# A new fixed instruction list for chunk-selected attention followed by an ELU MLP

## The chip, the core and the metric

The kernel runs on one core of a Trainium2 chip. A core has five instruction queues that run beside one another: TensorE (PE, matmuls), VectorE (DVE), ScalarE (ACT), GpSimd (POOL) and SyncE (SP, which here only starts DMAs). The metric is the device time of one execution in microseconds (us). Three runs of the kernel before took 292.13, 289.8 and 289.86, median 289.86.

## What is computed

The inputs are q, k and v, each 4 batches x 8 heads x 768 positions x 64 in float32, and two MLP weights, 512 x 2048 and 2048 x 512. The keys of a head are cut into 24 chunks of 32. A query sees only the 6 chunks whose upper bound is highest, among those that are not in its future:

```python
ub = np.sum(np.maximum(q * k_min, q * k_max), axis=-1)      # per query and chunk
ub = np.where(causal, ub, -1000000000.0)
top_chunks = np.argsort(ub, axis=-1)[..., -top_k:]
scores = scale * np.matmul(q, k.transpose(0, 1, 3, 2))
attn = softmax(np.where(mask, scores, -1000000000.0))       # mask: selected and not in the future
x = attn @ v                                                # heads joined to 512 columns
h = x @ w_in
g = np.where(h > 0.0, h, np.exp(np.minimum(h, 0.0)) - 1.0)
out = g @ w_out
```

## The kernel before, in words

The 3072 positions are worked off in eight units of 384. Units 0 and 1 hold the first and second quarters of batches 0 and 1 (192 positions of each batch); units 2 and 3 the second halves of these batches; units 4 to 7 the two halves of batches 2 and 3. A unit goes through preparation, selection, attention and the MLP.

Preparation (`prep_pair` L375, `prep` L519) loads keys and queries by DMA, turns them with matmuls against an identity (kT and qT, L403 for the first quarter units, L544 for the others), takes the least and greatest key of each chunk on DVE (kmin, kmax, L368), copies the turned keys and queries to where the score matmuls read them (kt, ka, qt, qa: the copy helper, L321 on ACT, L323 on DVE and POOL) and makes the positive part of the queries (qr, L343 or L345). Batches 2 and 3 take the bounds from a second load of the keys (`bounds_batch` L473: kc, kminc, kmaxc, kj on DVE at L485 to L500, then the transpose kw on PE at L507).

Selection (`select` L580) forms the upper bounds on PE (ub, L593), turns them on DVE (ubT, L604), finds the sixth largest of each query (max, L612), compares (lt, L617), turns the result back (sT, L621) and copies it as rows of mask beside the queries (mk, L321 on ACT, L323 on DVE and POOL). The first quarters see all their chunks and need no selection.

Attention (`attend_pair` L698, `attend` L760) has score matmuls (L721, L775), an exponential on ACT (ex, L728, L790, L794), a triangle of zeros and ones multiplied in on the diagonal (tri, L733, L807, on DVE or POOL), the weighted sums on PE (pv, L747, L826), and the division on DVE (rcp L637, on L639). The result is transposed for the MLP: on PE (px, L662, then a copy xt) in units 0 and 1, by a transposing DMA (xd, L650) in the others.

The MLP (`mlp` L837) has 16 first products a unit, each of four 128 x 384 matmuls into one PSUM bank (h, L844). Each is followed by an exponential on ACT (e, L851), one subtraction on POOL or DVE (m, L853) and a gate on DVE (g, L857). Twelve groups of four 128 x 512 matmuls (o, L865) make the output in three banks, which are copied out (oe, L321 on ACT or L323 on DVE) and stored by SP.

Nothing decides the order while the kernel runs. The operations are first recorded as a graph; `ORDER` (L39) is a written list of three-letter entries, the first letter the engine, the other two the number of the operation; `PLACES` (L103) gives the buffer numbers. The loop at L917 walks the list and issues each operation, so each engine's queue has the order of its entries. Waits between engines follow from the data and from the reuse of buffers, eight PSUM banks among them. Operations that can run on several engines (m, tri, mk, qa, ka, ky, oe and other copies) take the engine that their entry names.

```python
    with tc.manual_schedule():
        for j in range(0, len(order), 3):
            o = g.ops[64 * DIGITS.index(order[j + 1]) + DIGITS.index(order[j + 2])]
            ...
            o.emit({"P": PE, "A": ACT, "D": DVE, "G": POOL, "S": SP}[order[j]])
```

Fillers (L902) are matmuls of zeros against zeros, 256 columns wide, whose result nobody reads; 170 are recorded and the list names 33 of them. The list has PE 625 entries, ACT 476, DVE 469, POOL 242 and SP 155. The MLP weights are loaded by DMAs that POOL issues (w_in in three pieces, L292; w_out in four, L298), with their conversion to bf16.

Of the kernel before, what the change touches and what calls it, by code (L numbers as in the profile page):

```python
# [39 lines left out]
D00S0rA0sG09D01D03A0tS0yD0iA0WG0mS0wD0kA0uD0eD0qG0bS0vD0cG0aA0VG04S0xG05G0jPjRPjSPjTPjUPjVPjWP1j  # L40
A02P1yS0zP1oP1kG0lP0DS0XG0hP0TD0EG06S0YP0MD0HA0UG08G0oS0+G0fP0KD0NP11G0pD0FA0LA15D0OP1lS0BG0AD0Q
P1aA1nS2fD12P1pP1uA1mD17P1qD1cS0ZA1eP18D1bA0SP1hS2iG1gD13A19G0dA1iS2gP1tD0CA1sP1vGmwD10S2vP1NP1D
P1zA1xG0gP26P1AA1rA0JP25P1XP1EA0-S2ID27D28S2hA1wD1FP1SP1YD1GGmvA1BP1HS2PP1RP1IA1CP1OD1JP29G1dP1+
D1KG0GA0RGmxD1PA16G0nGmyS2OPjXPjYPjZPj-Pj+Pk0Pk1Pk2Pk3Pk4Pk5Pk6Pk7Pk8Pk9PkaPkbPkcP2BG14G1fP2aP1L
GmzD2bD2cP20P2oS2QD1TD21D1UP2dA2sD1ZD22A2FD1-A1MD1QD2tPkdPkePkfPkgP23D2HP1VD2pA24A2GD1WD2qA2ePm-
D0ID2CPmSAm+AmTPkhPkiPkjPkkPklP2JS2RDmUP2wDmVA2KD2DPmWA2LG2MD2rA2xGn0G0PDn1PmKG2EG2SD2yPmOPmGAmP
AmXPmCGmQA2uGmYP3lDmRAmHAmLG2zDmZPn2GmID3mGmMDmJPnyAn3GmAD3nAmDPnaDmNAnzD3pGmEPnuAbkG2AD3oAnbPnm
A2NGnAD3qPneG2jD3rS3fPniDn4S2kA3sDnBAnvDmFS2mP3HAnnGncDn5A3tPn6GnwDndAnjGnoP41A3vDnxPnPG07A42Dnp
GmBA3IDnkP3JP2XDnlA3KPnID2YAnfG3LD2+An7P4FP4DD2ZA4GPnqD3uDn8P3+AnrP4jDn9PnJA40GnsA4EGngP4lDntP38
A4mG4HDnhPnQS2TD31S32G30PnCD3aD39G2-P33P3gD34PnRS4+D3hA36G37S2VPnKA35D3iD3bA3cS50A4kP3wA3jG4nA3e  # L50
PnDD3yS4-A2nD3AG3kPnEA2UD3xG2lS4YD3zPnLG3dD3BG2WP4JD3CS4ZPnSAnMD3GA3ED3DD43P3NP3MS4XDnTP4MP4IP4a
A4ND3FP44D3OP45A4bD3PP4OS57P3QD46A4PP48PnFS7QA3RD4QA49D47S7OP3SP4sA3TP4oD4cP4pP4SA4tP4RP4uG3UShx
D4TP4dP5QD4UA4vP4eD4qP5fD4fG4wP3WD4gSnUP3VA5gP5rD3XA5RP4hD4KG5jS55P5EA5sD4LP4yG5iA4iP4xD3YP4VD4z
G5uP3ZD4AA4WP5xD4rA5FP58D5tA3-P4BD5yG5IP5kA5BP5JD4CG5HAnGD5mPoBG7RA5oD5cSnHPnZA5NG7PD5KS7SA5GPop
D5LA5OS7ND5aAn-PodA5UD5zS51Gn+Po1A5SD59G5TAoCDo0PoJAoqD5lGoDSaBAoePo5D5MG5AAo2D5nDoEGorPohA5eGof
S7UAoKPoxGo3A5pDogS5wPnVAo6DosGoLS7IAoyD5bDo4Po9Go7AoiS8hDoMA5hGozPolDo8AoaGojPotAnWDoASaFGobAom
DokP5VScPGnXA56DocGonAouS53DnYA52G5DDooScRPoFA5CG7TD5WPp6D5XGovAoGD5YG5qS7KPp7G5dD5ZGoHPo+SnOD5-
PoVSnNDowPoWD5+S7LPp0D60A61G62DoIPoXD5vP6gDaGP6cP6iA6hP6mP6eDaHP6lA6dPp8A6fDaJA6nP6aP64A6jPp1D54
G6oSaKA65D6kA6bP66P68P6yA67PoNA69A6zP6wP6qA6xP6GAoOP6pA6HP6uGoPPoRD6rA6vD6sG5PP6ADoQS6tAoSP74P6L
P6MDaIA6BP6IGoTA75P7aP79DoUPp9SazA6JA7bD6KS7MP6EA6NP6YD63P6CP76DpaA6FS7JPoYG6OA77DaLA6DG7cP6-P7A  # L60
P6QA6ZDaMG78A6+P70P6PAoZP6UP72D6RA71P6WSo-DaOP7zA73Pp2A6VSaXA7BP7uDp3P7wA6XP7oP7dG7CA7xD6SSp4P7s
P7mA7vDaNP7kSpbP7eA7lS6TG7yP8cD7fA7tP7qD7gP7iA7pP85D8dA7nP8uS7hA7jP7VD87G8gP8iA7rD86P7EA8yDbeP7D
# [891 lines left out]
```

## Time and profile before

| | before |
|---|---|
| median of three runs | 289.86 us |
| span of the profiled execution, first to last instruction | 287.8 us |
| what the median has beyond this span | 2.1 us |
| granted TensorE clock, mean of the core | 1.000 |
| HBM read and written | 30.41 MB and 6.29 MB |

The profiled execution's own time is known by its span alone; sums are made against the 287.8 us and the 2.1 us are added for the median. In the lines shown below, a group's row gives the line of the code, engine and operation, names and shapes, count, then busy time and the mean duration of one in ns, then the engine's idle time just before these instructions and what ended it. A row of the chain of waits gives start, length and what filled that piece of the path. A row of waits gives the engine and line that waited, what ended the wait, the total in us, how often, and the longest. A row of a DMA says how many KB it moved and the median time from issue to landing.

### The profile page before, as it was taken

What the parts mean: (1) busy time and instruction counts of PE and PEld (TensorE: products, weight loads), DVE (VectorE), ACT (ScalarE), POOL (GpSimd) and SP (SyncE); (2) the same over time, 40 slices, a digit from 0 to 9 for tenths busy, and PEclk for the clock granted to TensorE, in tenths of its full rate; (3) what the DMA queues carried; (4) which work ended last, traced back from release to release, by engine and by line L of the source; (5) the groups of instructions that cost most, each with busy time, mean ns of one, the idle gap of its engine ahead of it and who ended that gap; (6) DMA issues with size and microseconds to landing.
All of it is one profiled execution on the core that took longest, in us unless ns stands there. A gap on an engine that the chain in (4) does not pass through costs nothing.

```text
span 287.8 us, 6917 instructions
## 1 busy us (share of the span) xinstructions
PE 271.3 (94%) x2429; PEld 164.3 (57%) x2429; DVE 218.6 (76%) x637; ACT 213.4 (74%) x472; POOL 140.8 (49%) x271
## 2 busy tenths in 40 slices
PE   6998989999999879999798998999999999999995
PEld 3665555685465745567464544567555656565642
DVE  4628796879969999959898999747997698623850
ACT  2576786789499998889999449987886959891712
POOL 8483845277635668752387616620464135420400
PEclk9999999999999999999999999999999999999999
DMA  8999999939957699999753369604700220023102
GB/s 164 195 217 207 197 218 222 233 83 223 216 141 159 164 204 192 202 250 192 195 114 90 90 135 210 155 18 120 198 3 0 43 87 0 2 65 103 38 2 109
DMA packets 106963, 39.25 MB, mean 136 GB/s; under 512 B 98480, under 2 KB 102576, under 8 KB 106928
## 3 DMA queue, kind: packets, MB, share of 16 engines
q1 hardware_dynamic: 100464, 33.93, 57.1%
q0 software_dynamic: 3696, 4.19, 8.6%
q10 hardware_dynamic: 2768, 0.69, 1.3%
q8 instruction: 19, 0.31, 0.5%
q14 instruction: 16, 0.13, 0.2%
HBM read 30.41 MB, written 6.29 MB: 128 GB/s over the span
## 4 chain that ended last, share of the span: by engine, by line
PE 65%; DVE 20%; ACT 5%; DMA 4%; issue 3%; POOL 2%; DVEq 0%; POOLq 0%; ACTq 0%
PE bank L865 22%; PE bank L844 20%; PE bank L775 8%; PE bank L826 5%; DVE gT L857 4%; PE bank L403 2%; PE bank L593 2%; POOL m L853 2%; DVE thr L612 2%; DMA f<-in_q_dram 2%; DVE on L639 2%; PE bank L544 2%; ACT pt L790 1%; DVE kst L368 1%; DVE kn L494 1%
## 5 line engine op out<-in xcount | busy, mean ns | idle before, releaser
L865 PE MATMUL bank<-w_out_sb,gT 128*128 128x512 bf16 x384 | 92.3, 379 | 0.3 <-DVE gT L857 0.2
L844 PE MATMUL bank<-xt,w_in_sb 128*128 128x384 bf16 x512 | 89.5, 326 | 3.3 <-DMA xt<-on 1.8
L853 POOL TENSOR_SCALAR m<-e 128x384 f32<-128x384 f32 x107 | 56.2, 536 | 58.0 <-ACT e L851 47.7
L851 ACT ACTIVATE e<-bank 128x384 f32<-128x384 f32 x128 | 58.6, 492 | 19.4 <-PE bank L844 17.7
L844 PEld LDWEIGHTS <-w_in_sb 128*128 128x128 bf16 x512 | 49.3, 98 | 38.9 <-issue 7.3
L857 DVE SCALAR_TENSOR_TENSOR gT<-bank,m 128x384 bf16<-128x384 f32 x128 | 65.6, 549 | 7.7 <-POOL m L853 6.8
L790 ACT ACTIVATE pt<-bank 128x384 bf16<-128x384 f32 (+1 forms) x144 | 66.9, 545 | 4.5 <-PE bank L775 4.0
L865 PEld LDWEIGHTS <-gT 128*128 128x128 bf16 x384 | 36.3, 97 | 38.7 <-issue 2.7
L775 PE MATMUL bank<-rhs,lhs 96*128 96x384 bf16 (+2 forms) x240 | 44.1, 293 | 1.7 <-DVE gT L857 1.0
L807 POOL TENSOR_TENSOR pt<-pt,tri 128x256 bf16<-128x256 bf16 (+1 forms) x24 | 22.7, 958 | 28.3 <-ACT pt L794 18.7
L775 PEld LDWEIGHTS <-lhs 96*128 96x128 bf16 x240 | 21.3, 97 | 14.5 <-issue 1.4
L323 POOL CAST rhs<-qt 64x384 bf16<-64x384 f32 x29 | 15.1, 526 | 23.7 <-ACT qt L321 16.5
L637 DVE RECIPROCAL rcp<-bank 128x6 f32<-128x6 f32 (+1 forms) x40 | 7.4, 186 | 22.9 <-PE bank L826 13.0
L826 PEld LDWEIGHTS <-pt 128*128 128x128 bf16 x576 | 21.7, 97 | 4.2 <-ACT pt L790 0.5
L826 PE MATMUL bank<-vext,pt 128*128 128x65 bf16 x576 | 23.3, 193 | 0.1
L368 DVE TENSOR_REDUCE kst<-bank 128x12 f32<-128x384 f32 x32 | 16.7, 549 | 5.6 <-PE bank L403 3.7
L639 DVE TENSOR_TENSOR on<-bank,rcp 128x384 bf16<-128x384 f32 (+1 forms) x40 | 19.7, 501 | 1.3 <-PE bank L662 0.2
L321 ACT ACTIVATE o<-bank 128x512 f32<-128x512 f32 x14 | 8.5, 605 | 14.5 <-PE bank L865 14.5
L794 ACT ACTIVATE pt<-bank 128x512 bf16<-128x512 f32 x24 | 14.6, 617 | 3.0 <-PE bank L775 2.9
L321 ACT ACTIVATE rhs<-selT 32x384 bf16<-32x384 bf16 (+1 forms) x12 | 8.2, 682 | 9.1 <-DVE selT L621 8.9
L544 PE MATMUL bank<-ident_f,f 128*128 128x128 f32 x96 | 14.3, 276 | 0.6 <-DVE on L639 0.5
L321 ACT ACTIVATE rhs<-qt 64x384 bf16<-64x384 f32 x21 | 10.6, 519 | 3.4 <-DVE qt L323 3.2
(99 smaller groups left out, 328.8 us busy)
## 6 DMA issues: line engine op xcount, KB each, us to landing
f<-in_v_dram SPq DMA_DIRECT2D x22, 256.0 KB, 4.9
out_dram<-o SPq DMA_DIRECT2D x22, 256.0 KB, 2.4
f<-in_q_dram SPq DMA_DIRECT2D x18, 256.0 KB, 4.5
f<-in_k_dram SPq DMA_DIRECT2D x18, 256.0 KB, 4.6
kc<-in_k_dram SPq DMA_DIRECT2D x8, 384.0 KB, 4.4
w_out_sb<-in_moe_w_out_dram POOLq DMA_DIRECT2D x4, 512.0 KB, 12.0
f<-in_q_dram SPq DMA_DIRECT2D x6, 192.0 KB, 6.4
w_in_sb<-in_moe_w_in_dram POOLq DMA_DIRECT2D x2, 512.0 KB, 7.3
```

The lines of the kernel that those rows point to most:

```text
L321: nc.scalar.activation(out=dst, in_=src, func=AF.Copy)
L544: nc.tensor.transpose(ap(bk)[:, P * j:P * (j + 1)], ap(src[j])[:, P * r:P * (r + 1)], ident_f)
L639: g.op("on" + tag, (DVE,), lambda e: nc.vector.tensor_tensor(out=ap(on)[:, 0:nt].rearrange("p q h d -> p h q d"), in0=view()[:, :, :, 0:D] ...
L775: nc.tensor.matmul(ap(banks[hd])[:, o + pc:o + pc + wd], lhsT=apl(ls, G)[0:96, pr, hd, P * kb:P * (kb + 1)], rhs=ap(rs)[0:96, hd, c0 - HS ...
L790: lambda e, hd=hd, pt=pt, banks=banks, wtot=wtot: nc.scalar.activation(out=ap(pt)[:, hd, PAD:PAD + wtot], in_=ap(banks[hd])[:, 0:wtot], fu ...
L807: eng[e].tensor_tensor(out=view, in0=view, in1=tri[:, 64:64 + P].rearrange("p (a b w) -> p a b w", a=1, b=1) .to_broadcast([P, 2, len(dg), ...
L826: nc.tensor.matmul(view()[:, hd, qi, :], lhsT=ap(pt)[:, hd, P * qi + off:P * qi + off + P], rhs=ap(vx[b])[:, kb, 2 * r + hd, :], start=(kb ...
L844: nc.tensor.matmul(ap(bank)[:, 0:HS], lhsT=w_in_sb[:, kk, P * fc:P * (fc + 1)], rhs=ap(xT[i, kk]), start=(kk == 0), stop=(kk == NKK - 1))
L851: g.op(f"e{i}.{fc}", (ACT,), lambda e, eb=eb, bank=bank: nc.scalar.activation(out=ap(eb), in_=ap(bank)[:, 0:HS], func=AF.Exp), reads=[(ban ...
L853: g.op(f"m{i}.{fc}", (POOL, DVE), lambda e, eb=eb, mb=mb: eng[e].tensor_scalar(out=ap(mb), in0=ap(eb), scalar1=-1.0, scalar2=1.0, op0=AOT. ...
L857: nc.vector.scalar_tensor_tensor(out=ap(gt), in0=ap(bank)[:, 0:HS], scalar=0.0, in1=ap(mb), op0=AOT.max, op1=AOT.min),
L865: nc.tensor.matmul(ap(bank), lhsT=ap(gts[fc])[:, P * tt:P * (tt + 1)], rhs=w_out_sb[:, fc, :], start=(fc == 0), stop=(fc == NFC - 1))
```

## The change

Only `ORDER` and `PLACES` are replaced; every function, shape and number of buffers stays. The list was searched anew with operation times, semaphore delays and DMA landings that were read from a trace. The old list begins and ends so, and the new one below it:

```diff
 ORDER = """
-D00S0rA0sG09D01D03A0tS0yD0iA0WG0mS0wD0kA0uD0eD0qG0bS0vD0cG0aA0VG04S0xG05G0jPjRPjSPjTPjUPjVPjWP1j
...
-PwDDwtPwEPwKPwFPwLAwGSwHPwPAwMSwNPwQPwRAwSSwT
+S0xD00D0cS0uG0iA0tD03G04D09G0bG0oG0dS0vG0aD0eA0rD05S0sS0wP0DD0kD0ED0FP0MG0mPjUPjWD0OP0KD0LD0jD0H
...
+DvoSvpPvODwdAvPPw6DvQDvRAvXDvYDvZPwuPweAw7Gw8PwyDw9AwvGwwPv-Av+PwCDw0Dw1AwfSvBPwqAwrGwsDwtPwIDwg
+DwhPwOAwzPwDPwPAwjGwkDwlPwEDwAPwJPwKDwBDwxPwQPwFAwGSwHPwLDwMSwNPwRAwSSwT
 """
```

Read out, the two lists hold the same operations but for 23 fillers: 33 before, 10 after. Of the old fillers six stand first in PE's queue, 18 behind the first unit's weighted sums, four and five shortly after; of the new ones five stand among the first transposes, four more ahead of and within the first MLP unit, and one near the end of unit 2. Entries by engine are now PE 602, ACT 443, DVE 540, POOL 201 and SP 158. The engine of these operations changes:

| operation | before | after |
|---|---|---|
| m (subtraction in the MLP) | POOL 107, DVE 21 | POOL 86, DVE 42 |
| tri (triangle on the diagonal) | POOL 29, DVE 27 | POOL 19, DVE 37 |
| mk (mask rows) | ACT 12, DVE 12, POOL 8 | ACT 5, DVE 17, POOL 10 |
| qa (queries beside the mask) | POOL 29, DVE 6, ACT 21 | POOL 22, DVE 13, ACT 21 |
| ka (keys beside the chunk rows) | ACT 14, DVE 6, POOL 12 | ACT 7, DVE 7, POOL 18 |
| oe (output out of PSUM) | ACT 14, DVE 10 | ACT 10, DVE 14 |
| qr (positive part of the queries) | ACT 20, DVE 8 | ACT 17, DVE 11 |
| ky (one-hot rows) | POOL 6, ACT 5, DVE 1 | POOL 2, ACT 3, DVE 7 |
| first key loads | ACT 5, SP 23 | ACT 2, SP 26 |

One to three operations each of kb, ks, kt, kv, qh, v and vc move as well, and of the constants at the start identb, kp, kq, pz, rz and tnz go from POOL to DVE. The order within every queue is new too: nearly every line of PE's queue stands elsewhere than before.

More of the change, by code (lines that the diff above doesn't have):

```diff
@@ L45 @@
[L45 to L62, printed above, removed]
@@ L99 @@
[L99 to L101 removed]
+S0xD00D0cS0uG0iA0tD03G04D09G0bG0oG0dS0vG0aD0eA0rD05S0sS0wP0DD0kD0ED0FP0MG0mPjUPjWD0OP0KD0LD0jD0H
+D0QG0IPjYS0BG06G08Pj-D0GPjTD0NS0WP1kS0yP1jG0CP1oD0lD01P1lA1nA1mS0zG0AP0TP1tS0VP1aD1cS0XD0pS0+D10
+P11A15A0UP1pP1qA1rP1ES0YP1NP1hS2fD1iP18A19P1uP1vA1xD13D12D14D1eP1zA1wP1DD1FD1GS0ZA1sA0-S2gP2oD2p
@@ L119 @@
+28d41013033104027105601a13020217320c5100741645e501670345010612645023772140215620010612345230472
+03210161102g021025042b410d10214031752750019222a4210170437321230542c6100f12112127566714352661401
+0056131008154356240051623641075017602220310623203054117102e02043a101620dg502100173210b11f630221
+20507171422911c50222156012
 """
```

124 lines of the change are left out of this document (67 added, 57 removed).

## The prediction

> **What bounds the kernel now.** I read the page's busy shares first, then the chain of waits for the pace of each matmul group, then a table of busy time cut where one MLP unit's last second product begins, then the waits and the groups by line.
>
> ```profile
> span 287.8 us, 6917 instructions
> PE 271.3 (94%) x2429; PEld 164.3 (57%) x2429; DVE 218.6 (76%) x637; ACT 213.4 (74%) x472; POOL 140.8 (49%) x271
> PE 65%; DVE 20%; ACT 5%; DMA 4%; issue 3%; POOL 2%; DVEq 0%; POOLq 0%; ACTq 0%
> ```
>
> PE is busy for 94% and owns 65% of the chain, so it looks like the bound. Matmuls overlap, though, so busy time hides stalls. The pace is better read from the chain, whose rows give start, length and count:
>
> ```profile
> 199.99 1.34 PE bank L544 x12
> 219.65 1.31 PE bank L775 x12
> 229.10 1.45 PE bank L593 x32
> 248.45 0.92 PE bank L826 x30
> 263.44 10.40 PE bank L844 x64
> 273.84 10.37 PE bank L865 x48
> ```
>
> Unstalled, a first-product matmul (L844) takes 10.40/64 = 0.1625 us and a second-product one (L865) 10.37/48 = 0.216. I counted each list's matmuls, multiplied by such paces (L775 averages 0.13 over its widths), and call the sum PE content. The list before holds 258.4 us, of which 512 x 0.1625 + 384 x 0.216 = 166.1 is the MLP. The next table shows what the stages took; its columns are stretch, length, then busy time of PE, PEld, DVE, ACT, POOL, granted clock, DMA share, GB/s.
>
> ```profile
> 24.60:55.55 30.95, 29.48 (x280) 17.80 (x278) 25.18 (x81) 22.67 (x48) 15.73 (x32) 1.00 1.17 215
> 55.55:92.22 36.67, 36.32 (x354) 22.47 (x353) 31.30 (x97) 30.37 (x70) 21.16 (x37) 1.00 0.80 166
> 92.22:136.67 44.45, 41.53 (x427) 26.92 (x425) 39.58 (x108) 40.48 (x93) 27.11 (x48) 1.00 1.11 202
> 136.67:168.54 31.87, 28.94 (x257) 16.11 (x255) 29.28 (x80) 24.27 (x55) 18.90 (x30) 1.00 0.50 119
> 168.54:202.90 34.36, 33.39 (x298) 20.69 (x296) 26.48 (x82) 26.87 (x59) 13.02 (x22) 1.00 0.56 129
> 202.90:231.36 28.46, 28.46 (x259) 16.37 (x258) 22.99 (x69) 22.71 (x52) 11.28 (x22) 1.00 0.24 59
> 231.36:262.41 31.05, 31.05 (x281) 18.87 (x280) 19.99 (x63) 24.33 (x55) 12.46 (x18) 1.00 0.17 49
> 262.41:284.20 21.79, 21.79 (x117) 11.26 (x115) 10.85 (x26) 8.89 (x19) 3.50 (x7) 1.00 0.14 51
> ```
>
> PE content of these stages, u0 to u7, is 28.0, 35.1, 40.2, 27.8, 32.6, 28.1, 30.9 and 21.7. So PE loses 3.0, 1.6, 4.3, 4.1, 1.8, 0.4, 0.2 and 0.1 us in them, some 15 in all. Another 24.6 - 14.0 = 10.6 are lost ahead of the first MLP product, where PE waits for loads and is slow. The last four stages but u4 have almost nothing left to win. In u3 DVE is busy 29.28 of 31.87 us (92%), in u2 89%, in u1 85%: where PE stalls, VectorE is nearly full. Named stalls are few:
>
> ```profile
> PE bank L844 <- DMA xt<-on: 1.8, 1, 1.8
> PEld bank L507 <- DVE km L503: 2.1, 1, 2.1
> 99.74 2.42 DMA xt<-on
> ```
>
> **The change part by part.** Same operations, same buffers, a new order on all five queues and new slots; 2104 operations less unused fillers.
>
> *Fillers.* 33 become 10.
>
> ```profile
> 12.89 1.49 PE bank L403 x8
> 19.02 2.12 PE bank L904 x17
> 26.87 0.55 PE bank L904 x5
> 27.42 0.66 PE bank L403 x8
> ```
>
> Warm, a filler costs 0.55/5 = 0.11 us, so 23 fewer are 2.5 us of content (258.4 to 255.9). Six of the old ones stand first in PE's list and cost nothing; the 17 at 19.02 held the queue for 2.12 us, but partly while results of the first softmax were due. I take 1 us as won, between 0 and 2.5. The cover lost is the clock: eight 96-wide fp32 transposes took 1.49 us at 12.89 and 0.66 at 27.42, so PE ran at about half speed until some point between. If PE stayed slow up to the first product, the 6 us of content that falls between 16 and 24.6 would cost up to 6 more; nothing, if the waits swallow it. I take 0. The Trainium skill, "TensorE: Matmul & The Clock Gate", Part 1, says that PE starts at half clock and is released only after a window of about 3.4 us of steady activity, and is throttled again after as long an idle one. The trace agrees on the two paces; by that rule the missing fillers speak against the change, and the sum would be up to 289.6, an estimate.
>
> *Start.* Queue positions: the first key tiles go first on ScalarE (two loads there in place of five; three more on SyncE, so SP issues 26 of the key loads for 23). POOL reaches the second, third and first w_in loads after 7.1, 11.9 and 11.0 us of its own work against 9.8, 14.4 and 13.1, since tnz, kp, pz, kq, rz and the bf16 identity go to DVE, about 3 us there, half of it before any key has landed.
>
> ```profile
> 19.45 0.79 POOL L292 DMA_DIRECT2D w_in_sb<-in_moe_w_in_dram  x1
> 24.60 0.33 PE L844 MATMUL bank<-xt,w_in_sb 128*128 128x384 bf16 x1
> w_in_sb<-in_moe_w_in_dram POOLq DMA_DIRECT2D x1, 1024.0 KB, 12.8
> ```
>
> Issued at 19.45 and landed 12.8 later, at 32.25, that load held the eighth and later columns. 2.5 us less POOL work puts it at 29.8. PE content ahead of the first product falls from 14.0 to 12.5; DVE's content up to it rises by 4.7 us of busy time. I put the first product at 22.4 (24.6 less 2.2, the middle of 0 and 4.4: 1.5 content, 1 for keys that come first, up to 1.9 of waits), and, since h0.15 now follows 6.2 us behind it (28.6), a wait of 1.2 for w_in; PE's queue stands behind it, and ACT's exponentials wait for PE.
>
> *Work between engines.* By the two lists: m 21 from POOL to DVE; tri 10 the same way; mask copies 12 to 5 on ACT, 12 to 17 on DVE, 8 to 10 on POOL; qa 7 from POOL to DVE; oe 4 from ACT to DVE.
>
> ```profile
> L853 POOL TENSOR_SCALAR m<-e 128x384 f32<-128x384 f32 x107 | 56.2, 536 | 58.0 <-ACT e L851 47.7 <-DVE gT L857 6.6 <-DVE kc L494 0.7
> L853 DVE TENSOR_SCALAR m<-e 128x384 f32<-128x384 f32 x21 | 8.0, 390 | 5.6 <-ACT e L851 5.4
> L807 POOL TENSOR_TENSOR pt<-pt,tri 128x256 bf16<-128x256 bf16 (+1 forms) x24 | 22.7, 958 | 28.3 <-ACT pt L794 18.7 <-ACT pt L790 4.8 <-DVE pt L807 3.9
> L807 DVE TENSOR_TENSOR pt<-pt,tri 128x512 bf16<-128x512 bf16 (+1 forms) x24 | 9.6, 406 | 3.9 <-ACT pt L790 2.1 <-ACT pt L794 1.6
> L321 ACT ACTIVATE rhs<-selT 32x384 bf16<-32x384 bf16 (+1 forms) x12 | 8.2, 682 | 9.1 <-DVE selT L621 8.9
> L323 DVE COPY rhs<-selT 32x384 bf16<-32x384 bf16 (+1 forms) x12 | 4.6, 384 | 0.4
> L323 POOL CAST rhs<-qt 64x384 bf16<-64x384 f32 x29 | 15.1, 526 | 23.7 <-ACT qt L321 16.5 <-DVE qt L323 6.4
> L323 DVE CAST rhs<-qt 64x384 bf16<-64x384 f32 x6 | 2.5, 413 | 0.2
> L323 DVE COPY o<-bank 128x512 f32<-128x512 f32 x10 | 6.9, 686 | 2.9 <-PE bank L865 2.9
> ```
>
> DVE gains 21 x 0.390 + 10 x 0.406 + 5 x 0.384 + 7 x 0.413 + 4 x 0.686 = 19.8 us; small copies (ky, qr, qh, kt, v) about 5, the start's memsets about 3. DVE goes from 218.6 to about 246 us (by the means; the spread of m is shown next). POOL gives up 11.3 + 9.6 + 3.7 on the first three kinds, ACT 7 x 0.682 on masks; both had room. Each moved step is shorter (390 for 536 ns, 406 for 958), so a chain is shorter; but every step queued behind it on DVE is later.
>
> ```profile
> L853 POOL TENSOR_SCALAR m<-e x107: 501/510/1026, 28.8 to 272.6; 128x384 f32<-128x384 f32 x107
> L853 DVE TENSOR_SCALAR m<-e x21: 318/359/635, 27.4 to 276.5; 128x384 f32<-128x384 f32 x21
> ```
>
> Shortest, median and longest: some m take twice the shortest on either engine. If all 42 now on DVE took the longest, DVE would need 42 x (0.635 - 0.390) = 10.3 us more; at the shortest, 3.0 less. I keep the mean, for POOL has less to do. "SBUF — State Buffer", "Who interferes with whom", in the Trainium skill has a cause: DVE and GpSimd share a pair of SBUF ports, and a tensor_scalar in a two-port mode and a GpSimd instruction block one another in full, whoever comes second. The doubled longest values fit it; by it each m that meets a POOL instruction on DVE speaks against the move, up to those 10.3 us, an estimate.
>
> *Stage by stage.* By these means the busy time asked of DVE changes, u0 to u7, by 31.0/28.6, 42.5/37.7, 49.0/43.5, 36.5/36.3, 25.8/28.1, 34.9/25.7, 24.2/22.5 and 13.6/12.3 (sums of single durations, after over before). Times the table's DVE column: 27.3, 35.3, 44.6, 29.4, 24.3, 31.2, 21.5 and 12.0. PE content after: 27.0, 35.0, 40.0, 28.1, 31.6, 29.1, 30.9 and 21.7. DVE passes PE in u1, u2, u3 and u5. From below, packed instructions overlap:
>
> ```profile
> 36.78 2.18 DVE gT L857 x5
> L857 DVE SCALAR_TENSOR_TENSOR gT<-bank,m 128x384 bf16<-128x384 f32 x128 | 65.6, 549 | 7.7 <-POOL m L853 6.8
> ```
>
> five gates in 2.18 us are 0.436 each against a mean of 0.549, so a full DVE could need 10 to 20% less and PE would bind everywhere. From above, DVE keeps the 8% idle that it has in u3. I take the value between: the stage is the larger of PE content and scaled DVE, plus a remainder of 0.8 for masks that come just in time (0.4 where DVE already binds by much).
>
> *Stalls that go.* The transposing DMA into u2 is given 1.97 us of PE content between its last weighted sum and the first product, 0.98 before, when 1.9 were missing: 1.0 won. The bounds of the third batch (L507) get 12.2 us of PE content from their last key load, 9.2 before: 1.8 won. Late next: the last transposing DMA into u7 has 2.6 against 3.45 (0.3 lost), and mask copies now queue on DVE.
>
> The sum: 22.4 + (27.3 + 1.2) + 36.1 + 45.0 + 30.2 + 32.4 + 30.5 (u5: DVE's overhang runs on into u6, where it has room) + 31.0 + 21.8 + 3.6 from PE's end to the span's as before (287.8 - 284.2) = 281.5. The profiled span is 287.8 and the median 289.86; the 2.1 between is kept: 283.6.
>
> **The rivals.** (1) DVE packs fully: no scaled stage exceeds PE content, 0.8 stays in each of u0 to u6. 22.4 + 243.4 + 5.6 + 3.6 + 2.1 = 277.1. For it: the 0.436; against it: 92% busy in u3 went with 4.1 lost.
>
> (2) DVE becomes the bound, the slower end. If it keeps 8% idle, u0, u1, u2, u3, u5 cost 29.7, 38.4, 48.5, 32.0, 34.0; with 32.4, 31.0 and 21.8 elsewhere the total is 22.4 + 267.8 + 3.6 + 2.1 = 295.9. It decides from 95% busy in these stages downwards. For it: no stage of the list before has DVE above 92%; against it: its waits there were for POOL and ACT, which are relieved.
>
> (3) The change does not do what it says: DMA saturates the start anyway, other chains take the place of the named stalls, and only 1 us of filler goes: 288.9. For it: the third batch's waits move rather than vanish; DMA share is 1.17 in u0.
>
> (4) PE stays at half speed for the start: 283.6 + 3, half of the 6: 286.6 to 289.6.
>
> **How the numbers follow.** Forecast 0.48 (280 to 287), rival 1 0.14, rival 3 with 4 0.22, rival 2 0.16. A measurement of this kernel tells about 1% from no change, 2.9 us: under 287.0 is faster, over 292.8 slower. Faster 0.62, same 0.22, slower 0.16. The range runs from 275.0, under rival 1, to 292.0, at the foot of rival 2, leaving about 2 in 10.
>
> **What would show it.** Right: DVE near 245 us busy and POOL under 120; the first product near 22.4; the wait for xt under 1 us; none on L507; u1 near 36, u2 near 45. Wrong: u2 and u3 over 46 and 32 (rival 2), u1 to u3 at 35, 40 and 28 (rival 1), transposes at 0.19 us after 20 us (rival 4).

## The result

The changed kernel took 304.12 us in the median of four runs (301.79 to 306.0), the kernel before 290.59 in four runs beside it. The ratio is 1.0459, with a 95% interval of 1.0393 to 1.0525: slower by 13.5 us, where 283.6 was forecast. The time lies above the whole range. In five of the versions below, one or two of the four runs came out over 1.5% above the fastest of the same version; times and ratios there are those of the other runs, while the traces of the light triangles and of the two lists with all repairs are of such a slower run.

First the page of the changed kernel. Its line numbers are one lower than before (the expert's first product is L843 here, the output product L864).

```profile
span 302.4 us, 6820 instructions
PE 269.1 (89%) x2406; PEld 160.1 (53%) x2406; DVE 235.9 (78%) x709; ACT 199.5 (66%) x442; POOL 117.7 (39%) x229
PE 43%; DVE 33%; DMA 9%; ACT 6%; issue 5%; POOL 2%; SPq 2%; DVEq 0%; POOLq 0%; ACTq 0%
PEclk9999999999999959999999999999999999999999
```

The work went where the lists sent it: DVE up by 17.3 us of busy time, POOL down by 23.1, ACT down by 13.9. But the path left PE: it owned 65% of the chain before and owns 43% now; DVE went from 20% to 33% and DMA from 4% to 9%. No engine is fuller than 89%, so the new time is waiting. The 5 in the clock row is a slice of 7.6 us in which PE was granted about half its clock; before there was none.

The stages, cut where they were cut before (columns: stretch, length, busy time of PE, PEld, DVE, ACT, POOL, granted clock, DMA share, GB/s):

```profile
23.49:57.65 34.16, 28.64 (x260) 16.56 (x258) 27.84 (x91) 19.71 (x43) 15.32 (x27) 1.00 1.08 186
57.65:96.69 39.04, 36.12 (x359) 22.35 (x358) 34.03 (x102) 29.72 (x68) 19.71 (x35) 1.00 0.72 160
96.69:145.39 48.70, 44.78 (x425) 27.36 (x423) 41.72 (x126) 37.55 (x87) 19.06 (x33) 0.93 0.73 140
145.39:179.45 34.06, 29.80 (x260) 16.42 (x258) 29.95 (x109) 21.69 (x47) 11.54 (x20) 1.00 0.72 151
179.45:212.41 32.96, 32.01 (x288) 19.65 (x287) 25.39 (x64) 26.56 (x61) 12.37 (x19) 1.00 0.50 125
212.41:243.75 31.34, 30.08 (x268) 17.43 (x267) 28.24 (x83) 20.47 (x46) 11.03 (x20) 1.00 0.41 90
243.75:276.56 32.81, 31.20 (x281) 18.84 (x280) 20.40 (x65) 23.39 (x54) 12.31 (x19) 1.00 0.19 52
276.56:297.73 21.17, 20.97 (x113) 10.96 (x112) 10.79 (x24) 8.39 (x18) 4.56 (x9) 1.00 0.10 31
297.73:298.76 1.03, 1.03 (x5) 0.29 (x3) 0.69 (x1) 0.00 (x0) 0.00 (x0) 1.00 0.21 82
```

The last row is the rest up to PE's end, where the last stage was cut before; with it u7 takes 22.20 us. Against the kernel before, u0 to u3 lost 3.2, 2.4, 4.3 and 2.2 us, u5, u6 and u7 2.9, 1.8 and 0.4; the start won 1.1 and u4 1.4. VectorE is busy for 27.84/34.16 = 81% of u0, 87% of u1, 86% of u2, 88% of u3 and 90% of u5: full nowhere. In u3 it was busy for 92% before the change, in a shorter stage.

The waits say where PE stands (engine and line, what ended the wait, total us, times, longest). Two rows for PE, then one for DVE:

```profile
PE bank L843 <- DMA xt<-on: 6.4, 6, 1.6
PE bank L843 <- DMA w_in_sb<-in_moe_w_in_dram: 2.9, 2, 2.1
PE bank L543 <- DVE on L638: 1.9, 1, 1.9
```

```profile
DVE kst L367 <- ACT kt L320: 4.9, 4, 3.0
```

The wait for the transposed attention output was 1.8 us before, once; it is 6.4 in six places. Its pieces on the chain (start, length, what):

```profile
105.89 2.33 DMA xt<-on
146.06 4.27 DMA xt<-on x2
178.83 3.04 DMA xt<-on
242.40 4.11 DMA xt<-on
```

They stand where the first products of u2, u3, u4 and u6 begin. The first can be followed through three queues. ACT copies turned queries and keys out of PSUM (rows give start, length, operation, and in brackets the idle time before it with what ended it); then VectorE's queue, and PE's:

```profile
102.67 0.49 ACT L320 ACTIVATE qt<-bank 128x384 f32<-128x384 f32 x1 [1.02 <-PE bank L543]
103.33 0.87 ACT L320 ACTIVATE kt<-bank 128x384 bf16<-128x384 f32 x2 [0.16 <-PE bank L543]
```

```profile
100.70 0.55 DVE L367 TENSOR_REDUCE kst<-bank 128x12 f32<-128x384 f32 x1
104.23 0.56 DVE L367 TENSOR_REDUCE kst<-bank 128x12 f32<-128x384 f32 x1 [2.98 <-ACT kt L320]
105.05 0.18 DVE L636 RECIPROCAL rcp<-bank 128x6 f32<-128x6 f32 x1
105.27 0.56 DVE L638 TENSOR_TENSOR on<-bank,rcp 128x384 bf16<-128x384 f32 x1
```

```profile
102.80 1.15 PE L543 MATMUL bank<-ident_f,f 128*128 128x128 f32 x9
105.88 0.55 PE L543 MATMUL bank<-ident_f,f 128*128 128x128 f32 x3 [1.94 <-DVE on L638]
106.26 0.65 PE L843 MATMUL bank<-xt,w_in_sb 128*128 128x384 bf16 x3
108.26 8.36 PE L843 MATMUL bank<-xt,w_in_sb 128*128 128x384 bf16 x33 [1.34 <-DMA xt<-on]
```

ACT stood at qt112, which PE makes only after the last weighted sum; the copies kt111 and kt112 stand behind it. The reduce at 104.23 is kmax112. It reads the PSUM bank that kt112 reads, and stands behind that copy in the list, so it waits for it; and rcp013 and on013, whose input had been ready since 102.3, wait behind the reduce for 2.8 us. on013 holds the bank that the transpose kT110 needs (PE's 1.94 us at 105.88) and feeds the transposing DMA (1.34 at 108.26). Then the 33 expert matmuls take 8.36 us, 0.253 each, where 0.1625 is the pace without stalls: that is the clock's slice of 5.

The second, at the head of u3, is SP's:

```profile
140.89 2.00 SPq L304 DMA_DIRECT2D f<-in_v_dram  x2
142.94 2.39 SPq L467 DMA_TRANSPOSE lhs<-kt  x1
145.38 0.58 SPq L304 DMA_DIRECT2D out_dram<-o  x1
146.06 1.20 SPq L649 DMA_TRANSPOSE xt<-on  x1
147.30 0.58 SPq L304 DMA_DIRECT2D out_dram<-o  x1
147.99 1.20 SPq L649 DMA_TRANSPOSE xt<-on  x1
```

Two loads, a transpose of keys and two stores, none of them needed by this stage, stand ahead of and between the last two transposing DMAs that the expert's first products wait for.

### The profile page after: what moved, and what is told of

Read it like the earlier page. It is cut to its first block, busy times and chain, and to the rows that moved or that the text cites. A ratio compares the mean times of both kernels' runs of the same rounds, so it can differ in the third digit from the quotient of the medians.

```text
span 302.4 us, 6820 instructions
## 1 busy us (share of the span) xinstructions
PE 269.1 (89%) x2406; PEld 160.1 (53%) x2406; DVE 235.9 (78%) x709; ACT 199.5 (66%) x442; POOL 117.7 (39%) x229
## 3 DMA queue, kind: packets, MB, share of 16 engines
q1 hardware_dynamic: 102432, 34.42, 54.3%
## 4 chain that ended last, share of the span: by engine, by line
PE 43%; DVE 33%; DMA 9%; ACT 6%; issue 5%; POOL 2%; SPq 2%; DVEq 0%; POOLq 0%; ACTq 0%
PE bank L864 14%; PE bank L843 14%; DVE gT L856 8%; PE bank L774 6%; DMA xt<-on 5%; PE bank L825 4%; DMA f<-in_k_dram 3%; DVE thr L611 3%; DVE kst L367 2%; DVE rhs L322 2%; PE bank L543 2%; POOL m L852 2%; SPq L304 2%; DVE kc L493 2%; DVE m L852 2%
## 5 line engine op out<-in xcount | busy, mean ns | idle before, releaser
L843 PE MATMUL bank<-xt,w_in_sb 128*128 128x384 bf16 x512 | 93.8, 333 | 11.6 <-DMA xt<-on 6.4
L864 PE MATMUL bank<-w_out_sb,gT 128*128 128x512 bf16 x384 | 93.1, 379 | 1.3 <-DVE gT L856 1.0
L852 POOL TENSOR_SCALAR m<-e 128x384 f32<-128x384 f32 x86 | 44.1, 521 | 84.3 <-ACT e L850 57.2
L843 PEld LDWEIGHTS <-w_in_sb 128*128 128x128 bf16 x512 | 50.1, 99 | 49.3 <-issue 15.6
L856 DVE SCALAR_TENSOR_TENSOR gT<-bank,m 128x384 bf16<-128x384 f32 x128 | 67.0, 551 | 11.0 <-POOL m L852 8.9
L864 PEld LDWEIGHTS <-gT 128*128 128x128 bf16 x384 | 36.0, 97 | 39.5 <-issue 2.7
L806 POOL TENSOR_TENSOR pt<-pt,tri 128x512 bf16<-128x512 bf16 (+1 forms) x17 | 16.7, 989 | 40.1 <-ACT pt L793 23.8
L852 DVE TENSOR_SCALAR m<-e 128x384 f32<-128x384 f32 x42 | 15.8, 379 | 12.0 <-ACT e L850 11.7
L825 PE MATMUL bank<-vext,pt 128*128 128x65 bf16 x576 | 23.1, 193 | 1.2 <-DVE gT L856 0.9
L322 POOL CAST rhs<-qt 64x384 bf16<-64x384 f32 x22 | 11.8, 539 | 25.7 <-ACT qt L320 16.5
L806 DVE TENSOR_TENSOR pt<-pt,tri 128x256 bf16<-128x256 bf16 (+1 forms) x31 | 12.7, 415 | 6.3 <-ACT pt L793 5.2
L320 ACT ACTIVATE o<-bank 128x512 f32<-128x512 f32 x10 | 6.0, 601 | 15.0 <-PE bank L864 15.0
L402 PE MATMUL bank<-ident_f,f 96*128 96x96 f32 x64 | 9.4, 276 | 5.8 <-DMA f<-in_k_dram 5.5
```

The source lines that it names most:

```text
L806: eng[e].tensor_tensor(out=view, in0=view, in1=tri[:, 64:64 + P].rearrange("p (a b w) -> p a b w", a=1, b=1) .to_broadcast([P, 2, len(dg), ...
L825: nc.tensor.matmul(view()[:, hd, qi, :], lhsT=ap(pt)[:, hd, P * qi + off:P * qi + off + P], rhs=ap(vx[b])[:, kb, 2 * r + hd, :], start=(kb ...
L843: nc.tensor.matmul(ap(bank)[:, 0:HS], lhsT=w_in_sb[:, kk, P * fc:P * (fc + 1)], rhs=ap(xT[i, kk]), start=(kk == 0), stop=(kk == NKK - 1))
L852: g.op(f"m{i}.{fc}", (POOL, DVE), lambda e, eb=eb, mb=mb: eng[e].tensor_scalar(out=ap(mb), in0=ap(eb), scalar1=-1.0, scalar2=1.0, op0=AOT. ...
L856: nc.vector.scalar_tensor_tensor(out=ap(gt), in0=ap(bank)[:, 0:HS], scalar=0.0, in1=ap(mb), op0=AOT.max, op1=AOT.min),
L864: nc.tensor.matmul(ap(bank), lhsT=ap(gts[fc])[:, P * tt:P * (tt + 1)], rhs=w_out_sb[:, fc, :], start=(fc == 0), stop=(fc == NFC - 1))
```

## The experiments

Theory O: the loss is a handful of waits for single items, which in-order queues pass on, and goes when those items are moved. Theory L: the loss is VectorE's larger load, and moving items only moves the idle time. Later came theory C: idle stretches of PE cost again, through the granted clock. All edits of lists are read out in the names of the operations. Each ratio is to runs of the kernel before on the same chip; their medians were 290.37 to 290.68 us.

**The two halves alone.** The first run keeps the new order and gives each operation its old engine; the second does the reverse. By the two lists 239 operations change engine, 132 of them to VectorE and 61 away from it; the 71 of the expectation, like the moves told before, are the difference.

```diff
-D m0.3   # new order, as in the changed kernel
+G m0.3   # new order, engine of the kernel before; so for every operation whose engine changed
```

> The new list, entry for entry, but every operation on the engine that the old list gave it. Two theories of the 14 us. Theory L (load): the 71 entries moved to VectorE make its queue late, and all that waits on it; then giving them back brings the time to 290 plus or minus 3. Theory O (order): the new order leaves results too little time between the instruction that makes them and the one that needs them, whatever the engine; then this stays at 300 or above, for the order was laid out for the shorter durations on VectorE.

> The reverse: the old list, entry for entry, with the new list's engines. Theory L: 299 to 305, most of the loss without the new order. Theory O: 289 to 293, since the old order's gaps take up a busier VectorE.

They took 350.51 us (ratio 1.2061, 1.2008 to 1.2114) and 310.03 us (1.0669, 1.0618 to 1.0721). Neither L nor the bare sum of two effects: the halves cost 59.9 and 19.4 us alone and 13.5 together. An order is a plan for certain durations. With the old engines, VectorE does hardly more than before (219.2 us busy) and the kernel is the slowest of all: the gates on VectorE now stand behind steps that POOL does late, a wait of 8.9 us in the changed kernel. (A part of the 59.9 is the clock, which stood at half for 37.5 us of this trace.)

```profile
DVE gT L856 <- POOL m L852: 27.9, 34, 2.7
```

In the reverse run the chain of waits, of which VectorE owned 20% before, goes to VectorE:

```profile
DVE 40%; PE 38%; ACT 10%; issue 6%; POOL 3%; DMA 2%; POOLq 0%; DVEq 0%; ACTq 0%
```

**The fillers alone.** The kernel before, less 23 fillers.

```diff
-P fill   # 6 first in PE's queue, 17 of the 18 behind the first weighted sums
```

> The old list without 23 of its fillers (the first six and 17 of the next 18). If fillers carried the clock or the pace of the start, 292 to 296; if they only hold PE's queue, 288 to 290; either way this bounds what the filler part of the change can have cost.

It took 289.25 us, ratio 0.9952 (0.9918 to 0.9986). The fillers cost some 1.4 us and their cover was not needed at the start: the first product of the expert came at 22.14 (22.70 and 23.41 in two later runs with this start), before at 24.60.

**One reduce ahead.** The changed kernel; VectorE's kmax112 stands ahead of the copy kt112 in the list, beside kmin112.

```diff
 D kmin112
+D kmax112
 A kt112
-D kmax112
```

> The new list with one entry moved: VectorE's second reduce of a key bank in unit 2's preparation (kmax112) stands ahead of ScalarE's copy of the same bank (kt112), not behind it. In the trace of after, VectorE stood 3.0 us at that reduce for the copy, then the division on013 was late, then PE waited 2.1 and 1.6 us, then ran five groups at half pace (0.63 us each lost). If single waits of that kind cost the time (theory O, in its chain form), 304 falls to 296 to 300. If VectorE's load is what counts (theory L), it waits elsewhere instead: 302 to 304.

299.83 us, ratio 1.0317 (1.0249 to 1.0385): 4.3 us for one of 540 entries of VectorE's list, which did the same work as before. Of the later stages only u2 moved by more than 0.3 us:

```profile
97.00:140.32 43.32, 41.46 (x419) 26.29 (x422) 41.12 (x125) 36.87 (x86) 19.27 (x33) 1.00 0.82 158
```

48.70 became 43.32, VectorE is now busy for 41.12 of it (95%), and the clock is 1.00. A stage can hold that much DVE work with little loss; so 86% in the changed kernel was no ceiling. Of the 5.4 us, 2.5 are the two waits, in whose place one of 0.83 is left, and 3.0 the half clock that is gone. This speaks for O.

**Transposing DMAs ahead on SP.** The changed kernel, SP alone.

```diff
 S xd111
-S ldv310, ldv300, kd200, out1.2.0, xd112, out2.0.0, xd113
+S xd112, xd113, ldv310, ldv300, kd200, out1.2.0, out2.0.0
...
-S ldk302, ldq311, ldq301, xd200, xd202, xd201, ldv302, xd203
+S xd200, xd202, xd201, xd203, ldk302, ldq311, ldq301, ldv302
```

> The changed list with one edit: on SP, ldv310, ldv300, kd200 and the outputs of tiles out1.2.0 and out2.0.0 stand behind the transposing DMA xd113 in place of ahead of it, and ldq301, ldq311, ldk302 and ldv302 behind xd203. No engine's work changes. Theory O (named waits in the order): the waits of the first expert product at the fourth stage (2.62 us before h3.1) and at the fifth (1.12 us before h4.8) go, u3 falls from 34.06 to about 31.5 and u4 from 32.96 to about 32, and the whole time falls by 2.5 to 4 us against the changed kernel. Theory L (VectorE's load): its work is the same, so the time moves by 1 us at the most, and the idle time turns up at another place of the same stages.

301.37 us, ratio 1.0384 (1.0328 to 1.044): 2.7 us by the medians, as O said. PE's waits for the transposed output fell from 6.4 to 1.6 us (0.9 of that in u6, where the edit moves nothing), but u3 gave 1.5 in place of 2.5 and u4 0.2 in place of 1:

```profile
144.15:176.75 32.60, 29.32 (x258) 16.52 (x259) 29.08 (x109) 21.45 (x47) 10.62 (x20) 1.00 0.75 145
```

```profile
PE bank L843 <- DMA xt<-on: 1.6, 2, 0.9
PE bank L825 <- DVE gT L856: 2.2, 1, 2.2
```

The second row is a wait that was 0.9 us in the changed kernel: a weighted sum of u3 needs a PSUM bank whose content a gate on VectorE has still to read. So part of a won wait came back at VectorE, as L has it.

**The weights ahead on POOL.** PE waited 2.1 us for the third piece of w_in. Ahead of its issue stands oh, 3.4 us of work.

```diff
-G oh
 G w_in0
 G w_in2
+G oh
```

> The changed list with one edit: the operation oh on POOL (3.4 us there) stands behind the issue of the load w_in2 in place of ahead of it. Theory O: the 2.3 us that TensorE waits at h0.15 for that load's landing, and part of the 0.94 us at h0.1, go; u0 falls from 34.16 to about 32, the other stages keep their lengths within 0.3 us, the whole time falls by about 2 us. Theory L: u0 stays at 33.5 to 34.2, since VectorE's list of that stage is as long as before.

307.19 us, ratio 1.0618 (1.0537 to 1.0698): worse by 3 us. The wait for w_in went and u0 fell to 32.7. That is no gain of the edit: seven other traces of this section have the start of the changed kernel, and u0 takes 32.4 to 33.2 us in them. But the first product came at 27.7, in place of 23.5 (23.6 to 25.5 in those seven), for a query load that now landed late (window 20 to 30 us):

```profile
PE bank L402 <- DMA f<-in_q_dram: 3.4, 1, 3.4
```

The next three rows are the stretch from 8 to 33 us of the kernel before, the changed one and this one; the last two columns are the DMA share and GB/s:

```profile
8.00:33.00 25.00, 22.71 (x230) 15.28 (x229) 15.54 (x44) 15.99 (x35) 14.26 (x49) 1.00 1.26 204
```

```profile
8.00:33.00 25.00, 17.97 (x210) 10.99 (x207) 20.48 (x72) 13.79 (x28) 13.57 (x46) 1.00 1.25 211
```

```profile
8.00:33.00 25.00, 17.52 (x200) 11.57 (x200) 17.46 (x51) 12.61 (x25) 10.80 (x42) 0.93 1.21 206
```

All three move 204 to 211 GB/s at a DMA share over 1.2. The load that was moved ahead made another late, as it would if the transfers were the bound there. The end of u0 is at 55.55 before, 57.65 after (56.75 to 58.22 in the seven) and 60.41 here.

**All repairs at once**, the one on POOL included. To the three edits shown come two small ones:

```diff
 S ldv110, ldk110
-S out1.0.0
 S ldq112
+S out1.0.0
...
 D xts2
+D kmin011, kmax011
 D kmin010, kmax012, kmin012
-D kmin011, kmax011
```

> The changed list with every repair at once: kmax112 ahead on VectorE, the SP moves of e4, oh behind w_in2, the output out1.0.0 behind the load ldq112, and kmin011 and kmax011 directly after the second tile's xts on VectorE. Work and engines are as in the changed kernel. Theory O: the repairs add up, 4.3 (kmax112, measured) + 3 (SP) + 2 (w_in2) + 1 (bank of kt011) = 10 us, so about 294 us, which still leaves 3 us to the kernel before. Theory L: VectorE's 236 us is the same, so 299 to 301.

300.63 us, ratio 1.0355 (1.0283 to 1.0426); the forecast of 294 failed on the POOL edit. In the trace PE waits 4.8 us for the query load, the first product came at 31.4 and u0 ended at 65.1, 7.5 us late; from there on the kernel kept what the repairs had won. So it was run again without that edit:

> The changed list with the repairs of the last combination but without its edit at the start (oh stays ahead of w_in2): kmax112 ahead on VectorE, the loads and outputs behind xd113 and xd203 on SP, out1.0.0 behind ldq112, kmin011 and kmax011 directly after xts2. Theory O: what the single edits gave adds up, 4.3 and 2.7 us, so 297 us (295.5 to 298.5), with u2 near 43.3 and u3 near 32.5. Theory L: VectorE's work is unchanged, so what goes at one wait comes back at the next one of the same stage: 299 to 301, not under the 299.8 of the one edit.

296.62 us, ratio 1.022 (1.0181 to 1.026): the single gains add up, to 7.5 us, as O said. L's 299 to 301 lies outside the interval. In the trace u2 takes 44.17 us, near the 43.3 that was expected, but u3 34.42 and not 32.5: the wait for the gate is there, with the clock at half for 3.4 us behind it.

```profile
164.06 0.53 PE L825 MATMUL bank<-vext,pt 128*128 128x65 bf16 x12 [2.25 <-DVE gT L856]
```

**A lighter VectorE.** First the triangle where VectorE makes it, on 4 of 128 columns:

```diff
-                        out=view, in0=view,
-                        in1=tri[:, 64:64 + P].rearrange("p (a b w) -> p a b w", a=1, b=1)
-                        .to_broadcast([P, 2, len(dg), P]), op=AOT.mult)
+                        out=view[:, :, :, 0:n], in0=view[:, :, :, 0:n],
+                        in1=tri[:, 64:64 + n].rearrange("p (a b w) -> p a b w", a=1, b=1)
+                        .to_broadcast([P, 2, len(dg), n]), op=AOT.mult)   # n = 4 on DVE, else P
```

> The changed list, order and engines untouched; the multiplication by the triangle, where VectorE does it (31 of 48), works on 4 of its 128 columns, so most of the causal masking of those tiles is left out. That takes some 31 x 0.35 = 11 us of work from VectorE (235.9 us busy to about 225) and adds none elsewhere. Theory L: what VectorE is spared comes off the time nearly whole, 8 us or more. Theory O: the lists still wait at the same places (SP behind out1.0.0, the PSUM bank of kt112, w_in2), so the time falls by 0 to 3 us only.

300.62 us, ratio 1.0354 (1.0261 to 1.0447). That is 3.5 us, near O's 0 to 3 and far from L's 8, but the intervals of this run and of the changed kernel overlap, and the test was weaker than meant: VectorE's busy time fell by 5.0 us, not 11. So a heavier cut followed, in the minima and maxima of the key chunks, first in the changed kernel and then in the repaired one:

```diff
-                    out=ap(kc)[0:96, 0:512], in0=ap(kc)[0:96, 0:512], in1=ap(kc)[0:96, 512:1024], op=AOT.max),
+                    out=ap(kc)[0:96, 0:16], in0=ap(kc)[0:96, 0:16], in1=ap(kc)[0:96, 512:528], op=AOT.max),
...
-                        for n in (256, 128, 64):
-                            nc.vector.tensor_tensor(...)
+                        nc.vector.tensor_tensor(out=ap(km)[0:96, y, w], in0=ap(kc)[0:96, 0:64],
+                                                in1=ap(kc)[0:96, 64:128], op=op)
```

> The changed list, order and engines untouched; the running minima and maxima over the key chunks on VectorE (kminc, kmaxc: 28.5 us in all, of which 6.5, 7.3, 5.0, 6.9 and 2.8 us lie in u1 to u5) work on 16 or 64 columns in place of up to 512, so most of the bounds of the third and fourth batch is left out. Estimate of what VectorE is spared: 16 first steps from 0.7 to about 0.16 us and 16 second ones from 1.07 to about 0.3, 21 us in all, DVE busy 236 to about 215. Theory L: half of it or more comes off the time, 10 us or more, in u1 to u5. Theory O: the waits for single items stay where they are, and the time falls by 0 to 3 us.

> The list with the repairs of e10 and the lighter minima and maxima of e12 at once (the same part of the bounds left out). If after the repairs VectorE's load is the next bound, the lighter work gives much more here than alone: under 291 us. If single waits still set the time, it gives 0 to 3 us again: 294 to 297 us.

They took 301.23 us (1.0389, 1.035 to 1.0429) and 292.85 us (1.0104, 1.0083 to 1.0125). The page of the second:

```profile
PE 265.2 (91%) x2377; PEld 160.7 (55%) x2406; DVE 215.2 (74%) x677; ACT 198.5 (68%) x442; POOL 116.0 (40%) x229
```

| median us | the changed list | repaired |
|---|---|---|
| full work on VectorE | 304.12 | 296.62 |
| some 20 us less | 301.23 | 292.85 |

Twenty us of VectorE's work, which is less load than in the kernel before (218.6), win back 2.9 of 13.5 us, and 3.8 once the waits are gone. The second time lies between the 294 to 297 of pure O and the under 291 of pure L. VectorE's work counts, then, but for less than the waits; that it counts more once the waits are gone, 3.8 against 2.9, is within what runs of one kernel differ by. The kernel before was not run with the lighter work, so how much of the 3.8 us it would win too stays open. In the lighter repaired kernel u1, u2 and u3 take 36.28, 44.01 and 31.51 us, within 1.4 of the forecast of 36.1, 45.0 and 30.2; that is luck, for the forecast counted the full work.

**One wait filled.** The changed list with 14 zero matmuls inside PE's second wait of u2. Nothing else moves and no wait goes.

```diff
                 for kk in range(NKK):
+                    if i == 2 and fc == 3 and kk == NKK - 1:
+                        for _ in range(14):
+                            nc.tensor.matmul(ap(bank)[:, HS:HS + P], lhsT=zeros[:, 0:P], rhs=zeros[:, 0:P],
+                                             start=False, stop=False)
```

> The changed list, order and engines untouched; 14 matmuls of 128 columns on zeros stand in h2.3 ahead of its last product, on TensorE's wait of 1.61 us for xd013, in 128 columns of the bank that nothing reads; about 14 x 0.11 = 1.5 us of the wait are filled, and the results stay the same. Theory C (a stretch of idle TensorE is what brings the half pace after it): the groups h2.5 to h2.8 take 0.65 us again in place of 1.28, u2 falls from 48.7 to 45.5 to 46, and the whole time by 2 to 3 us, although no wait was taken away. Theory N (the half pace has another cause): the groups stay at 1.28 us and the time within 0.5 us.

301.13 us, ratio 1.0298 (1.0218 to 1.0378): 3.0 us by the medians, as theory C said, but its signs did not come. u2 fell by only 1.0 us in the profiled execution (47.67 after 48.70), and the half clock did not stay away. In the changed kernel it shows so (the third number from the right is the granted clock):

```profile
104.00:108.00 4.00, 1.03 (x6) 0.67 (x7) 3.70 (x10) 2.01 (x5) 0.89 (x2) 0.90 0.12 25
108.00:112.00 4.00, 3.74 (x12) 1.72 (x12) 3.22 (x9) 2.40 (x5) 1.53 (x4) 0.50 1.03 209
```

The 33 products that took 8.36 us there are given next for this run, then for the edit on POOL and the light triangles. Those two have the waits of the changed kernel at this place, 1.93 and 1.34 (1.33) us, with nothing in them:

```profile
108.81 6.15 PE L847 MATMUL bank<-xt,w_in_sb 128*128 128x384 bf16 x33
```

```profile
111.01 7.05 PE L843 MATMUL bank<-xt,w_in_sb 128*128 128x384 bf16 x33 [1.34 <-DMA xt<-on]
```

```profile
107.22 7.20 PE L844 MATMUL bank<-xt,w_in_sb 128*128 128x384 bf16 x33 [1.33 <-DMA xt<-on]
```

Read in steps of 1 us, the clock stood at half for 6.8 us in the changed kernel and for 3.4 us in each of these three. So a shorter half clock also comes without the filling, and that the filling shortened it is not shown. Where the rest of the 3.0 us comes from is open; the four runs lie between 298.24 and 303.29.

**The same in the kernel before.** If single waits count, the old list without its 23 fillers should have some to give. Three were chosen from its trace:

```diff
 P kT113
+P pv0131, pv0130
 P kT110, kT112
-P pv0131, pv0130
...
 D kmin111
+D rcp013, on013
...
 D sT20
+D mk203, mk202
...
 D on202
+D kminc301a   # stood ahead of rcp200
```

> The kernel before, its list and engines, without 23 fillers (289.25 us measured) and with three repairs of the kind found above: pv0131 and pv0130 ahead of kT110 on TensorE with rcp013 and on013 directly after kmin111 on VectorE, so that xd013 is issued about 1 us earlier (2.09 us of wait before h2.5); mk203 and mk202 directly after sT20 on VectorE (1.22 us of wait before sc20301); kminc301a behind on202 in place of ahead of rcp200 (1.6 us earlier for the transposing DMAs of the fifth stage, 0.91 us of wait before h4.5). Theory O: 1.0 + 1.2 and up to 0.9 us, 286 to 288 us, under both kernels. Theory L: VectorE's work is the same, so 288.5 to 290.

290.47 us, ratio 0.9999 (0.9977 to 1.0022): a miss. The fourth stage won (31.04 us after 31.87), the fifth did not (34.43 after 34.36), nor did the third, for the moved weighted sums met a PSUM bank that VectorE had not yet read, and PE's waits for the transposed output stayed as long as in the kernel before:

```profile
PE bank L843 <- DMA xt<-on: 1.9, 3, 1.4
PE bank L825 <- DVE qt L322: 0.9, 1, 0.9
```

So only the mask edit was kept:

```diff
 D sT20
+D mk203, mk202
 D kmaxc300a
```

> The kernel before, its list and engines, without 23 fillers (289.25 us measured) and with one edit: mk203 and mk202 directly after sT20 on VectorE. The fourth stage loses the wait of 1.2 us before sc20301, and the whole time is 288 to 289 us, a ratio of 0.992 to 0.995 to the kernel before. If instead the next wait of the stage takes its place, the ratio is that of the version without 23 fillers, 0.995 to 1.0.

289.16 us, ratio 0.9942 (0.991 to 0.9974). The fourth stage takes 31.23 us. It is the fastest version of this study, 0.6% under the kernel before, but it can't be told from the version that only drops the fillers (0.9952, 0.9918 to 0.9986).

## Why the prediction was wrong

The step that failed is the rule by which the stages were added: "the stage is the larger of PE content and scaled DVE, plus a remainder of 0.8". Its inputs were about right. It foresaw 27.3, 35.3, 44.6, 29.4, 24.3 and 31.2 us of VectorE in u0 to u5, and 27.84, 34.03, 41.72, 29.95, 25.39 and 28.24 were measured. (By its own figures VectorE passes PE in u0 too, 27.3 against 27.0; the text names u1, u2, u3 and u5 alone.) What no sum of busy times can see is the order within the queues: which item is at the head of SP, VectorE or PE, and what stands behind it. The remainder of 0.8 stood for that, with 1.2 for w_in in u0. Over the forecast inputs the lengths of u0 to u3 leave 3.7 to 6.9 us:

| us | first product at | u0 | u1 | u2 | u3 | u4 | u5 | u6 | u7 |
|---|---|---|---|---|---|---|---|---|---|
| forecast | 22.4 | 28.5 | 36.1 | 45.0 | 30.2 | 32.4 | 30.5 | 31.0 | 21.8 |
| after | 23.49 | 34.16 | 39.04 | 48.70 | 34.06 | 32.96 | 31.34 | 32.81 | 22.20 |
| repaired, lighter VectorE | 24.28 | 32.83 | 36.28 | 44.01 | 31.51 | 32.80 | 31.56 | 31.68 | 22.05 |

Point by point:

- *Fillers:* right. 1 us was taken as won; the fillers alone gave 1.4. The cover at the start was worth nothing, as taken. That an idle PE would lose its clock in the middle of the kernel (0.93 in u2) was not in the sum; rival 4 had it at the start. In the profiled execution of the changed kernel PE is not slow there: eight of the transposes took 0.88 us at 10.61. (The clock row alone would not tell, for it shows 1.00 at 12.89 in the kernel before too, where eight took 1.49.) But in five of the seven other traces with this start the clock fell to half for 3.4 or 6.8 us between 17 and 26 us; u0 ended at 57.1 to 58.2 in them and at 56.8 to 57.7 in the three without. So rival 4 was there in part, for about half a microsecond.
- *Start:* half right. The first product came at 23.5, not 22.4, but u0 ended at 57.65 and not at 50.9. The wait for the third piece of w_in was 2.1 us, not 1.2, and one of 0.8 for another piece came to it. The sum counted POOL's 2.5 us as that many for the landing; the landing came at about 33.3 and not at 29.8. The DMA share of 1.26 over the 25 us from 8 to 33 was in the trace of before and is what rival 3 named. Yet these waits do not set the end of u0: in the trace of the one reduce ahead there is none for w_in, and u0 ends at 57.74. Behind 33.4 us the chain of the changed kernel has no transfer in u0, but 12.6 us of VectorE and 2.4 of PE, where it had 10.6 and 11.1 before (from 30 us on). Which item in VectorE's queue costs u0 its time is open.
- *Work between engines:* right in kind. The named moves were put at 19.8 us, with small copies and the start's memsets about 27; the rise is 17.3, and POOL is under 120 as forecast. The named moves came to 18.3 by their rows, but work that stayed got shorter: the running minima and maxima of the key chunks took 32.4 us before and 28.6 after. The doubled durations that were feared did not come more often, as the row below shows: the mean of m on DVE is 379 ns, where it was 390. By the Trainium skill, "SBUF — State Buffer", "Who interferes with whom", the move might have cost up to 10.3 us; this trace shows nothing of that size.

```profile
L852 DVE TENSOR_SCALAR m<-e 128x384 f32<-128x384 f32 x42 | 15.8, 379 | 12.0 <-ACT e L850 11.7
```

- *Stalls that go:* one right, one wrong. No wait of the third batch's bounds for km is left. The transposing DMA into u2 was to win 1.0 us, because more PE content stood between the last weighted sum and the first product. But the content in between can itself be late: kT110 waited for a bank that on013 held. This wait and the next came to 3.3 us, and the half clock after them cost another 3 (33 matmuls at 0.253 in place of 0.1625). The forecast also named 0.3 us at the transposing DMA into u7; the waits came into u3, u4 and u6, which it had at nothing.
- *The rivals:* the sign was rival 2's, the mechanism only in part. It decided "from 95% busy" downwards, as if VectorE's idle share were a property of the engine. The one edit of kmax112 took u2 from 86% to 95% busy without a change of work. "Other chains take the place of the named stalls", in rival 3, comes nearest to what was measured, but it was priced at 288.9, as if they cost no more than the old ones.

The account of the 13.5 us by the runs: 7.5 are waits for single items outside the start, with the half clock behind them; 3.8 more come back with 20 us less work on VectorE; and 2.3 are left between the last version and the kernel before. The intervals of these times reach 0.6 to 1.9 us to either side, so the three shares are rough. In its stages the last version is longer than the kernel before in u0 (1.9), u5 (3.1) and u6 (0.6), against a gain of 1.6 in u4. 1.0 of u5 is PE content that the new order moved there from u4 by the prediction's count (28.1 to 29.1, and 32.6 to 31.6). The rest of u5 does not come from VectorE's load, for u5 kept its 31.56 us with 2.8 us less VectorE work; its cause is open. That the transfers bind the time up to the first product is argued from the DMA share and from the edit that only changed which load was late; a start with fewer bytes wasn't tried.

## What to carry to other kernels

In a fixed list for in-order queues, sum the work of a stage for its lower bound only; for the time, walk each queue and ask of every item that can be late what stands behind it, above all on the queue that issues DMAs. A list and its choice of engines are one plan: half of one with half of another was worse than either here. Where transfers come as densely as in the first 33 us here, moving one ahead can make another late by more. And an idle stretch of PE of about 2 us can cost twice, since half clock may follow it; as it comes in some executions and not in others, one trace of an edit does not show what the edit did to the clock.

## What the runs showed of the hardware

- Half clock follows waits of PE of about 2 us here, and not always. In u2 two waits of 1.94 (1.93) and 0.9 to 1.4 us, with 1.0 us of matmuls between, were followed by it in the changed kernel and in four other versions; the version with kmax112 ahead has one of 0.83 us there and the kernel before one of 1.8, and both kept 1.00. A single wait can do it too: in u3 one of 2.25 us did in the repaired list, while one of 2.16 at the same place, in the run with the transposing DMAs ahead, did not.
- Half clock comes in fixed lengths. Read in steps of 1 us, the traces of this study hold 28 stretches of it, without the last microsecond of a kernel: 17 of 3.4 us, ten of 6.8 and one of 20.5, six times 3.4. The Trainium skill, "TensorE: Matmul & The Clock Gate", Part 1, counts whole idle windows of about 3.4 us; the stretches agree with that length, but none of the waits above is as long.
- A transposing DMA holds SP for 1.2 us each, so four in a row need about 5 us of its queue (6.4 in u6), and its data came 2.3 to 5.0 us after issue in u2 and u3:

```profile
L649 SPq DMA_TRANSPOSE xt<-on x8: 1179/1204/1465, 96.9 to 148.0; - x8
DMA to landing us min/median/max: 2.3/2.8/5.0
```

- A reduce on VectorE waited 2.98 us for a copy on ACT though both only read the bank. The Trainium skill, "PSUM — Partial Sum Buffer", "PSUM bank collisions raise a hardware error", says that two engines must not access the same 32 partitions of one bank at once, reads against reads included, so by that page the wait is needed, both reading all 128. Which of the two goes first is free, and cost 4.3 us here.
